# Chunk attention and a wave MLP on one core: per-bank PSUM copies, single matmuls of zeros, more DMA transposes, and a new order of work

## The chip, the cores and the metric

The kernel runs on one core of one Trainium2 chip. The metric is device time in microseconds (us): the time of one launch, median over several runs. A profile of one execution is at hand for the kernel before the change. The engines go by these names: PE (TensorE, matmuls and transposes), PEld (its weight loads), DVE (VectorE), ACT (ScalarE), POOL (GpSimd, which here only issues loads) and SP (SyncE, which issues stores and DMA transposes). PSUM is the memory that PE writes to[...]. SBUF is the working memory.

## What is computed

The inputs q, k and v have the shape (8 batches, 8 heads, 576 tokens, 64). Attention runs within chunks of 64 tokens. Its output x (8, 576, 512) goes through a token-mixing layer and a channel layer:

```
scores = scale * q_c @ k_c.T          # per chunk of 64 tokens, per head
attn   = softmax(scores)
x      = attn @ v_c                   # heads side by side: (8, 576, 512)
theta  = x @ w_theta                  # 512 x 512
zr, zi = x * cos(theta), x * sin(theta)
y      = w_tok_r @ zr + w_tok_i @ zi  # mixing over the 576 tokens of a batch
u      = x + y
out    = u + relu(u @ w_ch)           # 512 x 512
```

## The kernel before

The work goes by pairs of batches, p = 0 to 3. The 2 x 576 tokens of a pair are nine tiles of 128 rows. Tiles 0 to 3 belong to the first batch, tiles 5 to 8 to the second, and tile 4 holds the last 64 tokens of each. Attention and theta go by groups: A is tiles 0 and 1, B is tiles 2 and 3, M is tile 4, C is tiles 5 and 6, D is tiles 7 and 8. The token mixing and everything after it go by single tiles.

The whole program is one hand-written list, ORDER (line 18), which the loop at line 569 walks from left to right. Each entry is step.place.slot, for example `H.1C.2`: theta of pair 1, group C, into PSUM slot 2. An entry such as `W.24.0` is pair 2, tile 4. [...] The steps are these:

- `q`, `k`, `v`: loads of one group, two DMAs each, issued by POOL (lines 174 and 182). They cast from float32 to float16. `lt` and `lc` load w_theta and w_ch, `lw.01` loads w_tok_i, all by POOL. `lw.00` loads w_tok_r by SP, and `cw` casts it on ACT. `init` makes the identity matrix on POOL, `ones` fills constants on DVE.
- `TW` transposes a third of the token weights on PE into two PSUM banks (line 225). `twd` copies part of it out on DVE, `twa` the rest on ACT (line 241).
- `T` transposes q and k of a group on PE into two PSUM banks (line 259). `tq` copies q out on DVE, `tk` copies k out on ACT, or on DVE for group M (lines 277 and 279).
- `S` is the scores on PE (line 290), `e` their exponential on ACT (line 303), `V0` and `V1` are attention times v for four heads each on PE (line 323), `v0` and `v1` the normalisation on DVE into x (lines 335 and 336).
- `X` transposes x on PE (line 354) and `x` copies it out on ACT (line 366). `Xd` (line 375) does both with one DMA transpose, issued by SP.
- `H` is theta on PE (line 388), `g` cosine and sine on ACT (lines 404 and 408), `z` the products on DVE (lines 417 to 426), `zm` two small DMAs on SP that bring the halves of group M to their places.
- `Y` is the token mixing of one tile on PE, nine matmuls of 128 x 512 (line 457). It needs z of the whole batch. `Ya`, `Yb` and `Yc` are parts of it. `y` adds x on DVE (line 465).
- `U` transposes u on PE (line 474), and `u` copies it out on ACT for even tiles and on DVE for odd ones. `Ud` (line 482) does both with one DMA transpose by SP.
- `W` is the channel layer on PE (line 497), `w` its relu and sum on DVE (line 506), `st` two stores by SP (line 521).
- `D` multiplies zeros by zeros on PE into one of two PSUM banks, twice (line 157). Its result is read by nobody.

The pool of x transposes holds three tiles, that of u transposes four, that of loaded q and k seven groups. [...]

Of the kernel before, what the change touches and what calls it, by code (L numbers as in the profile page):

```python
# [10 lines left out]
FP16 = mybir.dt.float16  # L11
# [4 lines left out]


ORDER = """
ones.00 D.00.0 lw.00 cw.00 D.00.1 init.00 D.00.0 D.00.1 q.0M q.0B q.0A D.00.0 k.0M
D.00.1 D.00.0 D.00.1 k.0B TW.00.0 twa.00 k.0A D.00.0 T.0M.1 tk.0M D.00.1 D.00.0 tq.0M  # L20
S.0M.2 e.0M lt.00 T.0B.1 T.0A.2 tk.0A tq.0B D.00.1 tq.0A tk.0B S.0A.2 v.0M V1.0M.1 v.0A
e.0A D.00.0 V0.0M.2 twd.00 S.0B.0 new.00 v1.0M V1.0A.1 v0.0M V0.0A.2 v0.0A v.0B q.1M
v1.0A lw.01 X.0M.2 e.0B V1.0B.0 X.0A.1 v1.0B x.0M H.0M.2 V0.0B.0 x.0A v0.0B q.0C k.1M
v.0C H.0A.1 g.0M X.0B.0 z.0M zm.0M x.0B g.0A TW.02.2 H.0B.0 T.1M.1 twa.02 twd.02 TW.01.2
z.0A Ya.01.1 tk.1M tq.1M g.0B Ya.03.0 twd.01 S.1M.1 k.0C q.0D z.0B q.1B twa.01 Yb.01
T.0C.0 e.1M Yb.03 tq.0C Yc.03 tk.0C S.0C.2 Yc.01 v.1M y.03 k.0D Ya.02.0 e.0C lc.00
V1.0C.1 new.10 V0.0C.0 Yb.02 y.01 v0.0C Yc.02 v.0D v1.0C U.01.1 X.0C.2 u.01 T.0D.0
V0.1M.1 Ya.00.1 Yb.00 x.0C tk.0D y.02 U.02.0 tq.0D v0.1M V1.1M.2 k.1B v1.1M S.0D.1
H.0C.0 u.02 W.02.0 w.02 e.0D V1.0D.2 q.1D V0.0D.1 Yc.00 v1.0D v0.0D g.0C U.03.0 T.1B.2
X.0D.1 X.1M.0 u.03 q.1A y.00 z.0C x.0D W.03.0 w.03 tq.1B x.1M U.00.1 k.1D u.00 H.0D.1  # L30
W.01.1 w.01 tk.1B g.0D z.0D H.1M.0 S.1B.2 k.1A g.1M T.1D.1 tk.1D q.1C v.1B tq.1D e.1B
v.1A W.00.0 k.1C w.00 z.1M Y.05.1 st.01 T.1A.0 tk.1A Y.07.0 v.1D y.05 tq.1A q.2D V0.1B.1
S.1A.2 S.1D.0 e.1D y.07 U.05.1 u.05 Y.06.0 U.07.1 v0.1B e.1A V1.1A.0 y.06 V1.1B.1 T.1C.2
u.07 tk.1C st.02 st.00 v1.1A U.06.0 u.06 tq.1C v1.1B st.03 Y.08.1 X.1B.0 v.1C V0.1A.2
x.1B S.1C.1 W.05.0 V0.1D.0 y.08 v0.1A e.1C v0.1D X.1A.2 x.1A w.05 U.08.1 zm.1M H.1B.1
W.07.0 H.1A.0 g.1B V1.1D.2 w.07 v1.1D Y.04.0 X.1D.1 q.2M z.1B k.2D q.2C g.1A V1.1C.2
T.2D.0 y.04 x.1D z.1A W.06.0 w.06 k.2M tk.2D H.1D.1 v1.1C st.05 u.08 Y.13.0 tq.2D S.2D.2
v.2C g.1D T.2M.0 k.2C y.13 V0.1C.1 Y.10.1 v0.1C X.1C.1 tk.2M tq.2M q.2A e.2D S.2M.0
st.06 T.2C.2 v.2D y.10 st.07 e.2M x.1C new.20 Y.11.0 q.2B v.2M z.1D q.3A W.08.1 tk.2C
k.2B tq.2C k.2A y.11 w.08 S.2C.0 V1.2D.1 U.11.0 e.2C v1.2D H.1C.2 u.11 V0.2D.0 v0.2D  # L40
V0.2M.1 q.3C g.1C U.13.1 v0.2M st.08 Y.12.0 u.13 W.11.1 y.12 X.2D.0 x.2D w.11 V1.2M.1
k.3A V1.2C.2 v1.2M W.13.0 v1.2C U.10.1 V0.2C.1 v0.2C u.10 T.2B.0 st.11 T.2A.2 tk.2A
tk.2B X.2M.1 w.13 tq.2A W.10.1 z.1C U.04.0 u.04 st.13 w.10 H.2D.2 x.2M k.3C tq.2B W.04.0
w.04 H.2M.1 g.2M Y.17.1 v.3C q.3M T.3A.0 X.2C.1 y.17 g.2D v.2B Y.14.0 st.10 z.2M S.2B.2
x.2C tk.3A tq.3A S.2A.1 S.3A.0 y.14 Ud.17 U.12.1 u.12 Y.18.0 y.18 e.2A Y.16.1 k.3M y.16
e.2B W.17.0 v.2A H.2C.1 e.3A w.17 V1.2A.2 v1.2A V0.2A.0 W.12.1 st.04 zm.2M Y.15.0 v0.2A
Ud.14 v.3D w.12 y.15 g.2C V1.2B.2 v1.2B V0.2B.0 v0.2B q.3B X.2A.1 W.14.1 x.2A Ud.18 w.14
st.17 U.16.0 u.16 T.3C.2 X.2B.1 W.16.0 w.16 tk.3C U.15.1 x.2B H.2A.0 u.15 q.3D k.3B
W.15.0 W.18.1 st.12 T.3M.1 k.3D tq.3C z.2C S.3C.2 w.15 w.18 z.2D tq.3M g.2A e.3C st.14
v.3A H.2B.0 Y.27.0 st.16 new.30 v.3M Y.28.1 z.2A tk.3M g.2B y.28 S.3M.2 y.27 z.2B  # L50
V0.3A.1 T.3B.0 Y.26.1 Y.20.0 tq.3B st.18 v0.3A tk.3B Ud.28 V1.3A.0 y.26 e.3M y.20 v1.3A
V1.3M.2 V1.3C.1 v1.3M v1.3C Y.24.1 V0.3C.0 T.3D.2 st.15 Ud.27 S.3B.1 y.24 tq.3D v0.3C
Ud.26 W.26.0 w.26 e.3B W.27.1 v.3B w.27 tk.3D V1.3B.1 V0.3B.0 v0.3B v1.3B S.3D.2 Ud.20
st.27 W.28.0 w.28 Y.21.1 y.21 Xd.3A Ud.21 Y.25.0 V0.3M.0 st.28 v0.3M y.25 e.3D V1.3D.2
V0.3D.1 st.26 Xd.3M Y.22.1 H.3A.0 Ud.24 v0.3D y.22 v1.3D W.21.0 w.21 W.20.1 H.3M.1 g.3A
Y.23.0 Ud.22 w.20 y.23 W.22.1 g.3M Xd.3B st.21 z.3M st.20 H.3B.2 Ud.25 g.3B Xd.3D W.24.0
w.22 w.24 W.25.1 H.3D.0 w.25 Xd.3C z.3B H.3C.1 z.3A g.3C Ud.23 W.23.0 st.22 w.23 z.3C
g.3D zm.3M Y.32.1 y.32 Y.31.0 z.3D Y.30.1 y.31 Y.37.0 st.24 st.25 y.30 st.23 Ud.30 y.37
Y.35.1 W.30.0 y.35 Ud.31 W.31.1 w.30 Ud.32 Ud.35 Ud.37 w.31 st.30 st.31 Y.36.0 W.35.1
y.36 w.35 W.32.0 w.32 st.35 Ud.36 Y.34.1 y.34 Y.33.0 W.37.1 y.33 W.36.0 w.37 Y.38.1  # L60
st.32 Ud.34 w.36 Ud.33 y.38 st.37 W.34.0 w.34 W.33.1 w.33 st.36 st.34 st.33 U.38.0 u.38
W.38.1 w.38 st.38 D.00.0
""".split()


# [1 line left out]
def kernel(  # L67
# [11 lines left out]
    nc = tc.nc  # L79
    B, H, S, D = q.shape  # L80
    DM = H * D
    CH = 64
    P = 128
    NDB = DM // P
    NE = H // 2
# [67 lines left out]

    def idle(p, i, slot):
        ps = psum1("ps_idle", slot)
        for r in range(2):
            nc.tensor.matmul(ps, blank[:, 0:P], blank, start=True, stop=True)

# [42 lines left out]

    def tok_w(k3, slot):
        ps = psum2("ps_wT", slot, FP16)
        for k in range(3):
            kt = 3 * k3 + k
            for tb in range(KT + 1):  # L210
                rows = slice(0, P if tb < KT else CH)
                if tb < KT:
                    at = k * KT * P + (tb // 2) * GT + (tb % 2) * CH
                    to = ps[:, at : at + GT].rearrange("p (c r x) -> p c r x", c=2, r=2)
                    to = to[:, :, 0]
                else:
                    at = 3 * KT * P + k * CH
                    to = ps[:, at : at + CH]
                for h in range(2):
                    if kt < 2 * KT:  # L220
                        ri, jl = kt // KT, kt % KT
                        s0 = (jl // 2) * GT + (jl % 2) * CH + h * P
                    else:
                        ri, s0 = h, KT * P
                    nc.tensor.transpose(
                        to[half[h]],
                        wnat[rows, tb, ri, s0 : s0 + CH],
                        id16[rows, rows],
                    )
        st["wT", k3] = ps  # L230

    def tok_w_copy(k3, r):
        ps = st["wT", k3]
        ks = slice(3 * k3, 3 * k3 + 3)
        most = ps[:, 0 : 3 * KT * P].rearrange("p (k x) -> p k x", k=3)
        if r == 0:
            c = slice(0, GT)
        else:
            c = slice(GT, KT * P)
        eng = nc.scalar.copy if r else nc.vector.tensor_copy  # L240
        eng(out=wT[:, ks, c], in_=most[:, :, c])
        if r == 0:
            eng(
                out=wT[:, ks, KT * P : S],
                in_=ps[:, 3 * KT * P : 3 * S].rearrange("p (k c) -> p k c", k=3),
            )

    def qk_t(p, g, slot):  # L250
        n = 1 if g == "M" else 2
        ps = psum2("ps_qkT", slot, FP16)
        psv = ps.rearrange("p (r w e j c) -> p r w e j c", r=2, w=2, e=NE, j=2)
        t = nats.pop((p, g))
        for w in range(2):
            for e in range(NE):
                for j in range(n):
                    for r in range(2):
                        nc.tensor.transpose(  # L259
                            psv[:, r, w, e, j, :],  # L260
                            t[half[r], w, j, 2 * e : 2 * e + 2, :].rearrange(
                                "s h d -> s (h d)"
                            ),
                            id16[half[r], half[r]],
                        )
        st[p]["ps_qkT", g] = psv

    def qk_copy(p, g, which):
        n = 1 if g == "M" else 2
        ps = st[p]["ps_qkT", g][:, :, which]  # L270
        name = "qk"[which] + "T"
        t = tmp.tile([P, 2, NE, n, CH], FP16, name=name, tag=f"{name}{n}", bufs=n + 1)
        st[p][name, g] = t
        copy = nc.scalar.copy if which and n == 2 else nc.vector.tensor_copy
        if n == 2:
            flat = "p r e j c -> p r (e j c)"
            copy(out=t.rearrange(flat), in_=ps.rearrange(flat))  # L277
        else:
            copy(out=t[:, :, :, 0], in_=ps[:, :, :, 0])

    def scores(p, g, slot):
        n = 1 if g == "M" else 2
        qT, kT = st[p].pop(("qT", g)), st[p].pop(("kT", g))
        ps = psum2("ps_sT", slot)
        psv = ps.rearrange("p (h j e c) -> p h j e c", h=2, j=2, e=NE)
        for j in range(n):
            for e in range(NE):
                for h in range(2):
                    for r in range(2):
                        nc.tensor.matmul(  # L290
                            psv[half[r], h, j, e, :],
                            kT[half[h], r, e, j, :],
                            qT[half[h], r, e, j, :],
                        )
        st[p]["ps_sT", g] = ps

# [306 lines left out]
```

The softmax here doesn't subtract the row's maximum and nothing guards it: scores larger than these inputs give would overflow.

## Time and profile before

| | |
|---|---|
| time, three runs | 213.17, 213.19 and 211.98 us (median 213.17) |
| the profiled execution | 213.03 us, its span 210.7 us |
| granted PE clock, mean over the span | 0.959 |
| busy: PE, DVE, ACT, POOL | 191.4, 123.6, 111.3, 104.4 us |
| loads by POOL (q, k, v) | 120 DMAs, about 0.87 us of POOL each |
| x transposes: by PE and ACT, by DMA | 15, 5 |
| u transposes: by PE and a copy, by DMA | 16, 20 |
| matmuls of zeros | 28 |

The profile is read in this way. Busy times are unions of an engine's instructions, and matmuls are pipelined: a 128 x 512 matmul has a duration of 0.38 us but in a stream one starts every 0.215 us. The span cut into slices shows which engine works when. The chain of waits that ended last is followed back from the last instruction; each of its pieces gives a start, a length and what ran. A table of waits says which instruction stood idle for which other. The table of DMA issues gives the time from issue to landing. Loads run from the start to about 120 us, and in that time the DMA engines are busy nine tenths or more in nearly every slice.

### The profile page before, as it was taken

Reading aid. Unit: us, or ns where it says so; the run is one execution under the profiler, and the core shown is the slowest. Engines: PE = TensorE matmul, PEld = TensorE weight load, DVE = VectorE, ACT = ScalarE, POOL = GpSimd, SP = SyncE. Lnnn points to the kernel's source line nnn. Section 1 sums busy time; section 2 is a strip of 40 time slices with the busy share of each in tenths; the row PEclk is TensorE's granted clock in tenths of the full one; section 3 lists DMA queues with packets and bytes.
Section 4 is the critical chain, followed back from the end, with each engine's and each line's share of the span. In section 5 each row is a group of like instructions: output and inputs, shape, how many; then the busy total and the mean of one; then the engine's idle time right before and its main releaser. Section 6 shows DMA issues by size and latency. Waiting matters only on the chain.

```text
span 210.7 us, 6370 instructions
## 1 busy us (share of the span) xinstructions
PE 191.4 (91%) x2774; PEld 96.7 (46%) x2774; DVE 123.6 (59%) x240; ACT 111.3 (53%) x119; POOL 104.4 (50%) x130
## 2 busy tenths in 40 slices
PE   7678698897989999999999999999899988999981
PEld 2334444353545654555555545545544424444430
DVE  0014644663959675776884447849886365846451
ACT  2525469635886668777567668793260631500010
POOL 8997889988999898987997000000000000000000
PEclk9965579999999999999999999999999999999999
DMA  6999999999999999999999972423428687626875
GB/s 191 189 149 171 186 156 159 162 157 156 150 147 210 218 160 178 153 213 158 169 186 201 190 106 53 104 50 65 91 56 173 125 173 151 151 59 130 174 155 130
DMA packets 136858, 31.36 MB, mean 149 GB/s; under 512 B 129536, under 2 KB 131648, under 8 KB 136832
## 3 DMA queue, kind: packets, MB, share of 16 engines
q0 software_dynamic: 114176, 15.88, 119.6%
q1 hardware_dynamic: 22656, 15.10, 31.5%
q8 instruction: 21, 0.34, 0.7%
q14 instruction: 5, 0.04, 0.1%
HBM read 33.06 MB, written 9.44 MB: 202 GB/s over the span
## 4 chain that ended last, share of the span: by engine, by line
PE 65%; DVE 9%; ACT 9%; DMA 7%; POOL 6%; issue 1%; SPq 0%; POOLq 0%; ACTq 0%
PE ps_y L457 27%; PE ps_theta L388 14%; PE ps_uw L497 13%; POOL qk L174 5%; DMA v<-in_v_dram 4%; PE ps_x L323 3%; DMA xT<-x 3%; ACT kT L277 3%; PE ps_qkT L259 3%; PE ps_sT L290 2%; DVE qT L277 2%; PE ps_xT L354 2%; DVE x L336 2%; ACT xT L366 1%; PE ps_uT L474 1%
## 5 line engine op out<-in xcount | busy, mean ns | idle before, releaser
L457 PEld LDWEIGHTS <-wT 128*128 128x128 f16 (+1 forms) x360 | 30.7, 100 | 34.4 <-issue 0.8
L457 PE MATMUL ps_y<-zr,wT 128*128 128x512 f16 (+1 forms) x180 | 44.4, 381 | 0.0
L457 PE MATMUL ps_y<-zi,wT 128*128 128x512 f16 (+1 forms) x180 | 42.0, 379 | 0.0
L465 DVE TENSOR_TENSOR u<-ps_y,x 128x512 f16<-128x512 f32 x36 | 24.7, 690 | 27.9 <-PE ps_y L457 27.8
L497 PE MATMUL ps_uw<-wch,uT 128*128 128x512 f16 x144 | 36.3, 380 | 1.2 <-ACT uT L491 0.7
L388 PE MATMUL ps_theta<-wtheta,xT 128*128 128x512 f16 x144 | 36.0, 393 | 1.4 <-DMA xT<-x 1.0
L174 POOL DMA_DIRECT2D qk<-in_q_dram x40 | 34.2, 875 | 4.9 <-issue 1.4
L174 POOL DMA_DIRECT2D qk<-in_k_dram x40 | 34.1, 870 | 2.7 <-DMA wnat<-in_moe_w_tok_i_dram 0.8
L182 POOL DMA_DIRECT2D v<-in_v_dram x40 | 34.1, 879 | 2.3 <-DMA qk<-in_k_dram 0.6
L506 DVE SCALAR_TENSOR_TENSOR o<-ps_uw,u 128x512 f32<-128x512 f32 x36 | 24.8, 689 | 15.8 <-PE ps_uw L497 15.5
L404 ACT ACTIVATE cos<-ps_theta,pihalf 128x1024 f16<-128x1024 f32 (+1 forms) x20 | 20.6, 1032 | 21.4 <-PE ps_theta L388 14.9
L303 ACT ACTIVATE eT<-ps_sT 128x1024 f16<-128x1024 f32 (+1 forms) x20 | 18.5, 939 | 16.9 <-PE ps_sT L290 16.8
L336 DVE TENSOR_TENSOR x<-ps_x,recip 128x512 f16<-128x512 f32 (+1 forms) x40 | 25.5, 638 | 1.4
L388 PEld LDWEIGHTS <-xT 128*128 128x128 f16 x144 | 13.7, 100 | 17.9 <-issue 2.1
L497 PEld LDWEIGHTS <-uT 128*128 128x128 f16 x144 | 13.0, 98 | 16.6 <-DMA uT<-u 1.3
L366 ACT COPY xT<-ps_xT 128x1024 f16<-128x1024 f16 (+1 forms) x15 | 13.9, 931 | 12.2 <-PE ps_xT L354 12.1
L277 ACT COPY kT<-ps_qkT 128x1024 f16<-128x1024 f16 x16 | 16.1, 1018 | 7.7 <-DVE qT L277 4.4
L408 ACT ACTIVATE sin<-ps_theta 128x1024 f16<-128x1024 f32 (+1 forms) x20 | 18.7, 937 | 0.0
L491 ACT COPY uT<-ps_uT 128x512 f16<-128x512 f16 x9 | 5.3, 592 | 24.3 <-PE ps_uT L474 24.2
L277 DVE COPY qT<-ps_qkT 128x1024 f16<-128x1024 f16 x16 | 11.0, 688 | 9.3 <-ACT kT L277 6.6
L259 PE MATMUL ps_qkT<-id,qk 64*128 64x64 f16 x576 | 12.8, 196 | 2.1 <-DMA qk<-in_k_dram 1.3
L335 DVE RECIPROCAL recip<-ps_x 128x8 f32<-128x8 f32 (+1 forms) x40 | 7.9, 197 | 10.5 <-PE ps_x L323 10.2
(43 smaller groups left out, 153.5 us busy)
## 6 DMA issues: line engine op xcount, KB each, us to landing
out_dram<-o SPq DMA_DIRECT2D x72, 128.0 KB, 2.4
qk<-in_q_dram POOLq DMA_DIRECT2D x32, 128.0 KB, 6.2
qk<-in_k_dram POOLq DMA_DIRECT2D x32, 128.0 KB, 6.5
v<-in_v_dram POOLq DMA_DIRECT2D x32, 128.0 KB, 6.7
wraw<-in_moe_w_tok_r_dram SPq DMA_DIRECT2D x1, 1152.0 KB, 5.8
wnat<-in_moe_w_tok_i_dram POOLq DMA_DIRECT2D x1, 576.0 KB, 7.7
qk<-in_q_dram POOLq DMA_DIRECT2D x8, 64.0 KB, 6.4
qk<-in_k_dram POOLq DMA_DIRECT2D x8, 64.0 KB, 6.1
```

The source lines that it names most:

```text
L174: nc.gpsimd.dma_start(nats[p, g][rows, which, r], (q, k)[which][b, :, t0 : t0 + n, :].rearrange("h s d -> s h d"),)
L182: nc.gpsimd.dma_start(v16[rows, slot + r, :, 0:D], v[b, :, t0 : t0 + n, :].rearrange("h s d -> s h d"),)
L259: nc.tensor.transpose(psv[:, r, w, e, j, :], t[half[r], w, j, 2 * e : 2 * e + 2, :].rearrange("s h d -> s (h d)"), id16[half[r], half[r]],)
L277: copy(out=t.rearrange(flat), in_=ps.rearrange(flat))
L336: nc.vector.tensor_tensor(out=st[p]["x"][:, j0 : j0 + n, f * NE * D : (f + 1) * NE * D].rearrange("p c (h d) -> p c h d", h=NE), in0=psv[: ...
L388: nc.tensor.matmul(ps[:, j * DM : j * DM + DM], xT[:, j * NDB + db, :], wtheta16[:, db, :], start=(db == 0), stop=(db == NDB - 1),)
L404: nc.scalar.activation(out=cos[:, 0:n].rearrange("p a e -> p (a e)"), in_=pin, func=AF.Sin, bias=pihalf, scale=1.0,)
L408: nc.scalar.activation(out=sin[:, 0:n].rearrange("p a e -> p (a e)"), in_=pin, func=AF.Sin)
L457: nc.tensor.matmul(ps[rows], wT[:, kt, cols], z[:, jz, :], start=(kt == 0), stop=(kt == 2 * KT),)
L465: nc.vector.tensor_tensor(out=u, in0=st[p].pop(("ps_y", j))[:, 0:DM], in1=st[p]["x"][:, j], op=ALU.add)
L497: nc.tensor.matmul(ps, uT[:, db * P : db * P + P], wch16[:, db, :], start=(db == 0), stop=(db == NDB - 1),)
L506: nc.vector.scalar_tensor_tensor(out=o, in0=st[p].pop(("ps_uw", j)), scalar=0.0, in1=u, op0=ALU.max, op1=ALU.add)
```

## The change

Five things change.

First, the copies out of PSUM go by bank. For groups A to D, `tq` now copies the bank of half r = 0 (q and k) on DVE, and `tk` the bank of half r = 1 (q and k) on ACT, into one common tile `qkT`. For group M one DVE copy takes both banks, and its `tk` is gone. The token weights are laid out in PSUM so that `twd` (DVE) reads only the first bank and `twa` (ACT) only the second.

Second, `D` is one matmul of zeros in place of two, and ORDER holds 60 of them in place of 14: 30 before the first `T`, 20 between it and the first `Y` part, one before `W.00`, and nine at the end behind `W.38`.

Third, x of pairs 1 and 2, groups A to D, is transposed by `Xd` in place of `X` and `x` (eight groups). Pair 3 was so before.

Fourth, u of tiles 0, 1, 2, 3, 5 and 6 of pair 1 is transposed by `Ud` in place of `U` and `u`.

Fifth, ORDER is written anew. It starts with groups A and B of pair 0 in place of M; `init` comes after ten loads; `cw` comes after the exponentials of groups A and B, and `TW.00` after the first attention; `lt` comes after 20 loads of q, k and v in place of 12; `lw.01` comes after 24 in place of 20. The other steps are the same in number.

The core of the diff, with ORDER cut to its beginning, a stretch of pair 1 and its end:

```diff
 ORDER = """
-ones.00 D.00.0 lw.00 cw.00 D.00.1 init.00 D.00.0 D.00.1 q.0M q.0B q.0A D.00.0 k.0M
-D.00.1 D.00.0 D.00.1 k.0B TW.00.0 twa.00 k.0A D.00.0 T.0M.1 tk.0M D.00.1 D.00.0 tq.0M
-S.0M.2 e.0M lt.00 T.0B.1 T.0A.2 tk.0A tq.0B D.00.1 tq.0A tk.0B S.0A.2 v.0M V1.0M.1 v.0A
...
+ones.00 q.0A D.00.0 D.00.1 q.0B D.00.0 D.00.1 D.00.0 D.00.1 D.00.0 D.00.1 D.00.0 D.00.1
...
+D.00.1 D.00.0 q.0M D.00.1 D.00.0 D.00.1 k.0A D.00.0 D.00.1 k.0B D.00.0 D.00.1 init.00
+T.0A.0 new.00 T.0B.1 tk.0A tq.0A lw.00 tk.0B k.0M tq.0B S.0A.2 D.00.0 S.0B.0 D.00.1
...
+v.1B V0.1A.1 v0.1A T.1B.0 tq.1B Y.04.1 tk.1B k.1C T.1C.2 tk.1C S.1B.1 e.1B zm.1M y.04
+tq.1C v.1C U.07.0 Xd.1A q.2M u.07 Y.06.1 q.2A U.04.0 V0.1B.0 y.06 V1.1B.2 S.1C.1 W.07.1
+u.04 v1.1B v0.1B Xd.1B U.08.0 u.08 w.07 H.1A.2 q.2C W.08.0 w.08 W.04.1 w.04 e.1C V0.1C.0
+V1.1C.1 Y.05.0 v.1D st.08 st.04 v0.1C k.2A V0.1D.0 g.1A V1.1D.2 v1.1C y.05 U.06.1 Xd.1C
+H.1B.1 U.05.0 u.06 W.06.1 v0.1D T.2A.0 g.1B z.1A k.2C v1.1D tk.2A new.20 w.06 T.2C.2
+H.1C.1 tq.2C st.07 u.05 g.1C Xd.1D z.1B q.2B W.05.1 Y.11.0 k.2M w.05 tq.2A st.06 st.05
+tk.2C v.2A H.1D.1 y.11 Ud.11 v.2M z.1C k.2B Y.10.1 y.10 g.1D S.2C.0 q.2D T.2M.2 W.11.0
...
+W.30.1 Y.38.0 w.30 y.38 Ud.24 W.34.1 W.24.0 w.34 U.38.1 u.38 st.30 W.38.1 w.24 D.00.0
+D.00.0 D.00.0 D.00.0 st.34 st.24 w.38 st.38 D.00.1 D.00.0 D.00.1 D.00.0 D.00.1
 """.split()
...
     def idle(p, i, slot):
         ps = psum1("ps_idle", slot)
-        for r in range(2):
-            nc.tensor.matmul(ps, blank[:, 0:P], blank, start=True, stop=True)
+        nc.tensor.matmul(ps, blank[:, 0:P], blank, start=True, stop=True)
...
     def tok_w(k3, slot):
         ps = psum2("ps_wT", slot, FP16)
...
+        first = ps[:, 0 : 3 * GT].rearrange("p (k x) -> p k x", k=3)
+        middle = ps[:, 3 * GT : 3 * GT + 3 * CH].rearrange("p (k x) -> p k x", k=3)
+        second = ps[:, 1024 : 1024 + 3 * GT].rearrange("p (k x) -> p k x", k=3)
+        for tbs in (range(KT), (KT,)):
...
     def tok_w_copy(k3, r):
-        ps = st["wT", k3]
+        first, middle, second = st["wT", k3]
         ks = slice(3 * k3, 3 * k3 + 3)
...
+            nc.vector.tensor_copy(out=wT[:, ks, 0:GT], in_=first)
+            nc.vector.tensor_copy(out=wT[:, ks, KT * P : S], in_=middle)
         else:
...
+            nc.scalar.copy(out=wT[:, ks, GT : 2 * GT], in_=second)
...
-    def qk_copy(p, g, which):
+    def qk_copy(p, g, r):
         n = 1 if g == "M" else 2
...
+        ps, t = st[p]["ps_qkT", g], st[p]["qkT", g]
+        if n == 1:
+            nc.vector.tensor_copy(
+                out=t[:, :, :, :, 0].rearrange("p r w e c -> p (r w e) c"),
+                in_=ps[:, :, :, :, 0].rearrange("p r w e c -> p (r w e) c"),
+            )
         else:
-            copy(out=t[:, :, :, 0], in_=ps[:, :, :, 0])
+            copy = nc.scalar.copy if r else nc.vector.tensor_copy
+            flat = "p w e j c -> p (w e j c)"
+            copy(out=t[:, r].rearrange(flat), in_=ps[:, r].rearrange(flat))
```

## The prediction

> **What bounds the kernel now.** I read the page's busy shares first, then the chain of waits in order of time, then the table of waits, then the DMA issues by stretch.
>
> ```profile
> PE 191.4 (91%) x2774; PEld 96.7 (46%) x2774; DVE 123.6 (59%) x240; ACT 111.3 (53%) x119; POOL 104.4 (50%) x130
> ...
> PEclk9965579999999999999999999999999999999999
> ```
>
> PE is busy nine tenths of the span; no other engine exceeds six. The second line is the granted clock in 40 slices of 5.3 us: it sags to half in the third to sixth. To see what PE's work is worth at full speed I take the pieces of the chain view in which PE follows PE: `Y` 1.94 us (2.05 for tile 4), `H` 1.73 (0.86 for M), `W` 0.86, `T` 0.57 (0.30), `S` 0.38 (0.20), `V` 0.25 (0.13), `X` 0.34 (0.17), `U` about 0.25, `TW` 1.54 from the timeline. Over ORDER, without zeros, this is 171.7 us. `W.38` ends at 205.9, so PE carries 34.2 us of **overhead** (idle, half clock, zeros). Where it arises: for a step, take its start in the timeline minus the full-speed work that stands before it.
>
> - `H.0M` starts at 25.5 with 5.4 of work before it: 20.1.
> - `S.1M` at 37.7: 23.2. `H.0C` at 50.1: 26.1. `S.1A` at 67.9: 27.3. `Y.17` at 111.9: 29.1. `Y.24` at 148.8: 30.7. `Y.32` at 179.0: 32.9. End: 34.2.
>
> So two thirds lie in the first 50 us, while loads arrive; afterwards PE is the bound and loses 8 us in 155. After `W.38`, 4.8 us remain to the end of the span (relu, store, closing).
>
> Two places show the reader how the losses look:
>
> ```profile
> 14.43 7.94 DMA v<-in_v_dram
> 22.41 0.66 PE ps_x L323 x28
> ...
> 47.35 0.92 ACT kT L277
> 48.29 0.69 DVE qT L277
> ...
> 171.23 3.25 DMA xT<-x
> 174.53 3.63 PE ps_theta L388 x16
> ```
>
> First PE waits for v to land. Then `S.0D` waits for the k copy and, after it, the q copy. Late in the run theta waits for a DMA transpose. The pair of copies is a wait of its own in the table (total us, times, longest):
>
> ```profile
> DVE qT L277 <- ACT kT L277: 6.6, 7, 1.4
> ...
> ACT kT L277 <- DVE qT L277: 4.4, 2, 3.5
> ...
> DVE wT L241 <- ACT wT L241: 3.6, 1, 3.6
> ```
>
> [...] weight loads of the zeros stand 0.43 us apart until 5.44 and 0.21 after; the clock is granted at 0.50 from about 12.7 to 28.7, in a stretch full of gaps. [...] two stores of a tile land in 2.4 us each after the loads, in 5.7 among them.
>
> **The change part by part.**
>
> *PE work removed.* Eight `X` by 0.34 and six `U` by 0.25: 4.2 us, leaving 167.5. PE is the bound from 50 us on, so this counts in full unless the transposes come late. The freed 8 x 1.01 us of ACT copies (line 366), 3 x 0.59 of ACT and 3 x 0.42 of DVE copies (lines 491 and 489) are worth nothing by themselves: ACT is at 53%.
>
> *Copies by bank.* Sizes are unchanged (0.69 on DVE, 1.02 on ACT), but they start together: `T` to `S` is shorter by the 0.69 that stood behind. For M, one copy of some 0.69 replaces two of 0.42. On PE's path I find this pair before `S.0C` and `S.0D` (idle 0.84 and 1.29), and near 107, 117 and 145; I take 1.4 us in 38 to 50, 0.6 in 68 to 112, 0.4 later. In the token weights it frees 1.5 to 3.6 us of waiting on ACT and DVE, partly on the path to the first `Y`.
>
> *The start.* POOL begins loads at 0.75 (before: 1.43, after the identity). Ten loads at 0.86 later `init` costs 0.5. `v.0A` is issued by 11.6, and with 6.7 to land comes near 18.3, not 22.4. But `lt` now stands behind 20 loads: 0.75 + 0.5 + 20 x 0.86 = 18.5, and it took 7.6 from issue to landing (11.45 to 19.05), so `H.0M` cannot start before 26.1: overhead 20.7 there, 0.6 more than before. `lw.01`, four loads later relative to attention, is issued near 23.5 and lands (7.5) near 31; `TW.01` has 10.6 of work ahead, at overhead 21 or more 31.6, so it is just in time. The cast `cw` (2.1 + 0.7 on ACT) was free in the load wait; now `e.0M` stands behind it, ending near 21, and `V1.0M`, `TW.00` and `X.0M` still precede 26.1. So `lt` is what is late next. By `S.1M` I take 23.2 again: the bank copies and a sooner full clock win back the 0.6.
>
> *Zeros.* 30 before the first `T` cost 10 x 0.43 + 20 x 0.215 = 8.6 us and end near 10, before k lands near 12: covered. Twenty among the first steps cost 4.3 us warm, 8.6 cold; between 12 and 26 PE has only 5.4 us of work, so I count nothing; without that cover, up to 8.6. One later: 0.2. Nine behind `W.38`: the first four precede nothing, the next needs the bank that `w` reads until 206.6, then five take 1.1 us, inside the store's 2.4: nothing.
>
> *DMA transposes.* Each `Xd` puts 1.28 us of issue on SP, each `Ud` 1.21: 17.5 us on a queue that spends far more than that waiting between 60 and 120. Behind a waiting `Xd` stand stores, and for them `w`, which has four output tiles; `Ud` too. The stretch is the loaded one:
>
> ```profile
> out_dram<-o SPq DMA_DIRECT2D x16, 128.0 KB, 5.7
> ...
> uT<-u SPq DMA_TRANSPOSE x1, 6.6
> ...
> xT<-x SPq DMA_TRANSPOSE x5, 3.2
> ```
>
> These are stores between 60 and 100, the first `Ud` at 114.6, and all `Xd` of before, which ran after the loads. A loaded `Xd` isn't shown. From below it is 3.2; by ratio of stores 3.2 x 5.7 / 2.4 = 7.6, and I allow 10. I take what load adds to a store, 3.3: 6.5. For `Ud` 5.1 and 6.6 are shown; I take 5.7. Against that stands the PE work between the last `V` and `H`, with 0.9 us per normalisation on the way: 1A 0.9 + 6.5 against 8.25; 1B 1.8 + 6.5 against 8.38; 1C 8.3 against 6.92; 1D 8.3 against 9.01. `Ud.11`: 0.9 + 5.7 against the 4.35 between `Y.11` and `W.11`; `Ud.10` 6.6 against 6.12, covered by 11's stall. Others have 6 us after the loads, or 10. Stalls: 1.4 + 2.25 = 3.6 us. At 3.2 and 5.1, the bound from below: 1.6. At 10 and 6.6, stalls inside another's interval counted once: 10.6.
>
> *Loads.* Their number and 0.87 us each stay; pairs 2 and 3 are issued 5 to 30 us ahead of use, so a few us of DMA time for the transposes cost nothing. If the cover goes, pair 1's loads are nearest (`k.1A` lands near 50 to 53, used at 54).
>
> *Late transposes of pair 3* stay: `Xd.3B` to `Xd.3D` still follow each other on SP; 2.2 us of loss kept.
>
> **Sum.** Overhead 20.7 at `H.0M`; 2.5 to `S.1M`; 1.5 to `H.0C` (2.9 less 1.4); 1.2; then 1.8 - 0.6 + 3.6 = 4.8 for 68 to 112; 1.2 (1.6 less 0.4); 2.2; 1.3: 35.4. With 167.5 and 4.8 the span is 207.7, against 210.7. The profiled execution was 213.03, 2.3 more than its span and 0.1 under the median, so **210.0 us**.
>
> **Rivals.** *Transposes in time and an early full clock.* Stalls 1.6, and the half clock until 28.7 is gone (theta and attention from 25.5 to 30.3 took 2.5 us more than at full speed; I take 1.5): 3.5 less, 206.5. For: sustained zeros at the front. Against: POOL's landings of 6 to 7 us.
>
> *Transposes too late (slower).* At 10 and 6.6 the stalls are 7.0 more: 217. For: the DMA engines show nine tenths until 120, and x's 256 KB are twice u's. It decides from where stalls exceed 6.6, near a loaded `Xd` of 8.2. Its place is `H.1A` to `W.11`, 70 to 100 us.
>
> *A late start.* PE stays at half clock, zeros of 0.43 lie in front of real work, and `lt` lands at 28: 3 to 4 more, 213.5.
>
> *The banks change nothing*, because ACT's 1.02 is what `S` waits for: the 2.4 us counted return, 212.4.
>
> **How the numbers follow.** About 1% is what a measurement can tell from no change. Forecast 0.36 (0.24 of it faster, 0.12 the same); in time and warm 0.24, all faster; late start or no effect of the banks 0.14 (0.02 faster, 0.09 same, 0.03 slower); transposes too late 0.26 (0.03 same, 0.23 slower). Together faster 0.50, same 0.24, slower 0.26. The range 204 to 217 leaves out some 0.08 below and 0.11 above; the forecast's own is 207.5 to 212.5.
>
> **What would show it.** In the changed profile: q and k copies on ACT and DVE that start together; `H.0M` near 26, held by wtheta; the clock at full before 28; `Xd` of pair 1 landing in 6 to 7 us; PE idle before `H.1C` and `W.11`, 1 to 3 us each; overhead near 35. I am wrong if loaded `Xd` take over 8 us, if loads wait for transposes and `T` of pair 1 or 2 waits for k, or if `H.0M` starts after 28.

## The result and the profile after

The changed kernel takes **233.22 us** (median of four runs, 231.06 to 233.91) against 212.6 us before: a ratio of 1.095, 95% interval 1.087 to 1.104. It is slower by a tenth, outside the range of 204 to 217. The profiled execution took 233.91 us, its span is 232.1. Ratios and their intervals, here and below, leave out runs that took over 1.5% longer than the fastest run of the same kernel.

The page of the changed kernel (busy shares, granted clock in 40 slices of 5.8 us, shares of the chain that ended last):

```profile
PE 197.4 (85%) x2654; PEld 95.6 (41%) x2654; DVE 122.0 (53%) x233; ACT 96.5 (42%) x104; POOL 104.2 (45%) x130
...
PEclk9967999999999799599799599999999999999999
...
PE 51%; DMA 25%; ACT 10%; DVE 8%; issue 3%; SPq 2%; POOL 0%; ACTq 0%; DVEq 0%; POOLq 0%
```

PE has fallen from 91% to 85%, and DMA holds a quarter of the chain (7% before). The clock reaches full sooner, and sags again four times between 75 and 133 us. The chain in order of time (start, duration, what) says where:

```profile
69.32 8.85 DMA xT<-x
...
78.21 3.12 PE ps_theta L392 x8
...
86.00 8.13 DMA xT<-x
...
94.17 3.60 PE ps_theta L392 x8
...
102.15 7.08 DMA uT<-u
...
109.28 1.74 PE ps_uw L501 x4
111.02 2.92 PE ps_y L461 x9
...
119.66 10.18 DMA uT<-u
...
129.88 1.89 PE ps_uw L501 x4
131.77 2.79 PE ps_y L461 x9
```

Each line with DMA is a transpose that PE waits out. Over the matmuls behind these four waits the granted clock averages 0.59, 0.50, 0.63 and 0.62, and the first piece behind each takes about twice its time at full speed. At full speed the six PE pieces here take 1.73, 1.73, 0.86, 1.94, 0.86 and 1.94 us: 7.0 us lost at the lower clock. PE's idle time in these four waits and in that of `H.2D` is 2.54, 3.65, 3.54, 5.75 and 2.20: 17.7 us.

The DMA issues between 60 and 100 us (queue, count, KB, median us from issue to landing):

```profile
out_dram<-o SPq DMA_DIRECT2D x11, 128.0 KB, 6.5
qk<-in_q_dram POOLq DMA_DIRECT2D x9, 128.0 KB, 8.5
v<-in_v_dram POOLq DMA_DIRECT2D x8, 128.0 KB, 10.3
qk<-in_k_dram POOLq DMA_DIRECT2D x8, 128.0 KB, 9.5
...
xT<-x SPq DMA_TRANSPOSE x4, 8.9
```

Not only the transposes are late. In the same stretch of the kernel before, stores landed in 5.7 us and the loads in less time too:

```profile
qk<-in_q_dram POOLq DMA_DIRECT2D x11, 128.0 KB, 6.8
v<-in_v_dram POOLq DMA_DIRECT2D x12, 128.0 KB, 6.4
qk<-in_k_dram POOLq DMA_DIRECT2D x12, 128.0 KB, 7.0
```

The last load's issue ends at 135.5 us instead of 114.9 (timeline of the changed kernel, then of the one before):

```profile
133.73 1.76 POOL L183 DMA_DIRECT2D v<-in_v_dram  x2 [0.31 <-DMA qk<-in_q_dram]
```

```profile
114.01 0.88 POOL L182 DMA_DIRECT2D v<-in_v_dram  x1 [0.19 <-issue]
```

POOL's own waits say why; waits of its load instructions for earlier loads of q, k and v sum to 22.6 us, before to 4.0. The largest two (us in total, times, longest):

```profile
POOL qk L175 <- DMA qk<-in_q_dram: 11.2, 7, 3.7
POOL qk L175 <- DMA v<-in_v_dram: 6.8, 5, 2.5
```

**The banks.** In the waits of the changed kernel the two copies of q and k still wait for each other, and its timeline shows them in turn:

```profile
DVE qkT L283 <- ACT qkT L283: 19.5, 7, 13.9
...
ACT qkT L283 <- DVE qkT L283: 8.3, 4, 4.1
```

```profile
69.08 0.68 DVE L283 COPY qkT<-ps_qkT 128x1024 f16<-128x1024 f16 x1
...
69.84 1.93 ACT L283 COPY qkT<-ps_qkT 128x1024 f16<-128x1024 f16 x2 [4.13 <-DVE qkT L283]
...
71.80 0.69 DVE L283 COPY qkT<-ps_qkT 128x1024 f16<-128x1024 f16 x1 [1.30 <-ACT qkT L283]
```

Each starts as the other ends, though they read different banks.

**Overhead** (start of a step minus the full-speed work ahead of it) is 22.8 at `H.0M` (28.2 us), 23.2 at `S.1M`, 24.3 at `H.0C`, 26.9 at `W.07` (74 us), 31.2 at `W.06`, 41.1 at `W.11`, 52.7 at `W.14` (151 us), 58.3 at the end. The loss lies mainly between 74 and 151 us.

### The profile page after: what moved, and what is told of

The parts are those of the page before. It is cut to its first block, busy times and chain, and to the rows that moved or that the text cites. A ratio compares the mean times of both kernels' runs of the same rounds, so it can differ in the third digit from the quotient of the medians.

```text
span 232.1 us, 6142 instructions
## 1 busy us (share of the span) xinstructions
PE 197.4 (85%) x2654; PEld 95.6 (41%) x2654; DVE 122.0 (53%) x233; ACT 96.5 (42%) x104; POOL 104.2 (45%) x130
## 4 chain that ended last, share of the span: by engine, by line
PE 51%; DMA 25%; ACT 10%; DVE 8%; issue 3%; SPq 2%; POOL 0%; ACTq 0%; DVEq 0%; POOLq 0%
PE ps_y L461 23%; DMA uT<-u 11%; PE ps_uw L501 11%; PE ps_theta L392 8%; DMA xT<-x 7%; PE ps_idle L158 3%; DMA qk<-in_q_dram 3%; DMA qk<-in_k_dram 3%; ACT qkT L283 2%; DVE x L340 2%; ACT cos L408 2%; ACT sin L412 2%; PE ps_x L327 2%; DVE qkT L283 2%; PE ps_qkT L259 1%
## 5 line engine op out<-in xcount | busy, mean ns | idle before, releaser
L501 PE MATMUL ps_uw<-wch,uT 128*128 128x512 f16 x144 | 39.4, 404 | 12.0 <-DMA uT<-u 11.1
L461 PEld LDWEIGHTS <-wT 128*128 128x128 f16 (+1 forms) x360 | 31.7, 102 | 37.6 <-issue 4.7
L461 PE MATMUL ps_y<-zr,wT 128*128 128x512 f16 (+1 forms) x180 | 46.0, 392 | 0.0
L392 PE MATMUL ps_theta<-wtheta,xT 128*128 128x512 f16 x144 | 37.2, 404 | 8.4 <-DMA xT<-x 8.4
L408 ACT ACTIVATE cos<-ps_theta,pihalf 128x1024 f16<-128x1024 f32 (+1 forms) x20 | 20.6, 1031 | 30.2 <-PE ps_theta L392 29.3
L283 ACT COPY qkT<-ps_qkT 128x1024 f16<-128x1024 f16 x16 | 16.1, 1015 | 27.9 <-PE ps_qkT L259 19.6
L392 PEld LDWEIGHTS <-xT 128*128 128x128 f16 x144 | 13.7, 102 | 26.7 <-DMA xT<-x 10.2
L283 DVE COPY qkT<-ps_qkT 128x1024 f16<-128x1024 f16 x16 | 10.9, 686 | 19.9 <-ACT qkT L283 19.5
L158 PE MATMUL ps_idle<-blank 128*128 128x512 f16 x60 | 19.4, 460 | 1.4 <-DVE blank L145 1.2
L495 ACT COPY uT<-ps_uT 128x512 f16<-128x512 f16 x6 | 3.5, 587 | 33.1 <-PE ps_uT L478 33.1
L259 PE MATMUL ps_qkT<-id,qk 64*128 64x64 f16 x576 | 12.6, 195 | 4.4 <-DMA qk<-in_k_dram 2.9
L259 PEld LDWEIGHTS <-qk 64*128 64x128 f16 x576 | 10.3, 97 | 9.0 <-issue 4.9
```

Source lines behind the costliest of these rows:

```text
L259: nc.tensor.transpose(psv[:, r, w, e, j, :], t[half[r], w, j, 2 * e : 2 * e + 2, :].rearrange("s h d -> s (h d)"), id16[half[r], half[r]],)
L283: copy(out=t[:, r].rearrange(flat), in_=ps[:, r].rearrange(flat))
L392: nc.tensor.matmul(ps[:, j * DM : j * DM + DM], xT[:, j * NDB + db, :], wtheta16[:, db, :], start=(db == 0), stop=(db == NDB - 1),)
L408: nc.scalar.activation(out=cos[:, 0:n].rearrange("p a e -> p (a e)"), in_=pin, func=AF.Sin, bias=pihalf, scale=1.0,)
L461: nc.tensor.matmul(ps[rows], wT[:, kt, cols], z[:, jz, :], start=(kt == 0), stop=(kt == 2 * KT),)
L501: nc.tensor.matmul(ps, uT[:, db * P : db * P + P], wch16[:, db, :], start=(db == 0), stop=(db == NDB - 1),)
```

## Experiments

Times are medians of all runs; the kernel before was 212 to 213 us beside every one of them.

**1. All fourteen transposes back on TensorE, then one kind alone.** In the new order, each `Xd` or `Ud` gives way to the pair of steps that it replaced, put where a PSUM tile is free:

```
-tq.1C v.1C U.07.0 Xd.1A q.2M
+tq.1C v.1C U.07.0 X.1A.0 x.1A q.2M
...
-H.1D.1 y.11 Ud.11 v.2M z.1C k.2B Y.10.1 y.10
+H.1D.1 y.11 v.2M z.1C k.2B Y.10.1 U.11.0 u.11 y.10
```

> The changed kernel with x of pairs 1 and 2 and u of six tiles of pair 1 transposed on PE again (14 transposes taken from the DMA queue, put back on PE with their copies). Theory LATE (PE waits for transposes that land late among the loads, and its clock drops in the waits): the 23 us of overhead beyond the forecast go, 4.2 us of PE work return: 210 to 215, most likely 211. Rival ORDER (the new order of the rest, the zeros or the copies by bank make it slow): 225 or more.

> Only the eight x transposes go back to PE; the six of u stay on the DMA queue. LATE: the waits before theta (about 8.4 us of PE idle with the clock loss behind them 12) go and those before W stay, though shorter since fewer transposes share the queue: 216 to 223. ORDER: 228 or more.

> Only the six u transposes go back to PE; the eight of x stay. LATE: the two waits before W (9.3 us of PE idle, with the clock loss about 13) go, those before theta stay: 217 to 224. The two halves, e2 and e3, should together give about the whole of e1. ORDER: 228 or more.

Measured: both back 220.62 (ratio 1.039, 1.033 to 1.044); X alone back 224.88, 229.14 and 229.83, too far apart for an interval; U alone back 227.21 (1.067, 1.061 to 1.073). All three missed the ranges. The transposes account for 12.6 of the 20.6 us. By the fastest of its runs X alone gives back 8.3, and U alone gives back 6.0, together a little more than both; whether the two kinds simply add up is not shown. And some 8 us remain with these fourteen back on TensorE.

**2. The same transposes, read by nobody.** As both-back, with the fourteen issued at their places as well, into dead space:

```
+    def x_extra(p, g):
+        t = spare(1024).rearrange("p (a c) -> p a c", c=P)
+        nc.sync.dma_start_transpose(t, st[p]["x"][:, j0 : j0 + 2].rearrange("p a e -> p (a e)"))
```

> X and U are computed on TensorE as in e1_xu_pe (220.6 us), and the same fourteen DMA transposes are issued as well, at the places they have in the changed kernel, into a space that nothing reads. So nothing waits for a transpose, but they still take DMA time from the loads. Theory LATE (the matmuls wait for the transposes' landing; the loads are hardly touched): 219-223, and no idle time of TensorE over 1 us before H.1A, H.1C, W.11, W.13. Theory CROWD (the transposes' descriptors hold up the loads of q, k, v and what follows them): 225 or more, the loads ending near 136 us as in the changed kernel rather than near 115.

Measured: 232.47 (1.097, 1.089 to 1.104), as slow as the changed kernel, with no matmul waiting for any of the fourteen. The last load's issue ends at 135.0. POOL's largest wait for earlier loads of q, k and v without and with them:

```profile
POOL qk L175 <- DMA v<-in_v_dram: 1.9, 2, 1.1
```

```profile
POOL qk L176 <- DMA qk<-in_q_dram: 9.4, 6, 3.8
```

So the presence of the transposes costs, and waiting for their landing is only one form in which it is paid. Where PE paid here, its timeline shows (the idle time ahead of the instruction and what ended it in brackets):

```profile
118.50 0.64 PE L462 MATMUL ps_y<-zr,wT 128*64 128x512 f16 x2 [2.88 <-issue]
```

```profile
152.34 1.89 PE L517 MATMUL ps_uw<-wch,uT 128*128 128x512 f16 x4 [3.43 <-DMA uT<-u]
```

The second is a transpose that both-back has too, now late. The first stands in the middle of a group, waiting for nothing that these views show; it comes back at the same matmuls with 0.9, 1.5 and 2.0 us in the next experiments and not in both-back. The traces also keep each DMA packet, and those of the queue that the page calls `instruction`, some 21 pieces of 16 KB in a run, tell more. One such piece landed at 117.04, 1.46 us before PE went on. The kept traces have 18 pauses of PE over 0.4 us without a releaser, in eleven kernels, and each of them ended 1.36 to 1.74 us after such a piece had landed. In both-back the piece landed at 111.62, and PE passed the same place at 113.3 without a pause. The piece itself took 1.63 us, 1.00 in both-back. That PE had run out of instructions there, because this transfer was late like the others, is an inference from these times and from the queue's name; no run tested it. Behind the pause PE ran slower: the granted clock was 0.50 until 123.8 us and 0.65 until 129.6.

At the end this trace has 12.6 us more overhead than that of both-back. Of these, 2.1 are there at `W.07` (76.8 us), 1.3 of them before the first added transpose. From there to 109 us both grow alike, by 5.0 and 4.9. Then 7.0 come until 130 us, the pause of 2.88 and the lower clock behind it, and 3.6 with the late transpose at 152. The changed kernel lost about as much in other places, so it is partly chance that the two times agree so closely.

**3. Is it the bytes, the small packets, the transposing, or the place?** Three variants of the last: the fourteen moved to later places, meant to be behind the last load (with x of pair 2 as source); plain copies of the same bytes; plain copies in pieces of 256 bytes.

```
-        nc.sync.dma_start_transpose(t, st[p]["u", j])
+        nc.sync.dma_start(t, st[p]["u", j].rearrange("p (b c) -> p b c", c=P))
```

> As e4_xu_pe_added (232.5 us: X and U on TensorE, and fourteen DMA transposes of the same sizes that nothing reads), but the fourteen are issued one by one between about 125 and 160 us, after the loads of q, k and v have ended; their source is x of pair 2. Theory CROWD (they cost because they take DMA time from the loads): 219-224, the last load issued near 119 us as in e1_xu_pe (220.6). Theory QUEUE (they cost because of SyncE's queue and of the stores and transposes behind them, wherever they stand): 229 or more.

> As e4_xu_pe_added, at the same places, but the fourteen are plain copies of the same bytes within SBUF in place of transposes; nothing reads them. Theory BYTES (what costs is the bytes that they move): 229 or more, the last load near 133 us. Theory FORM (the transposing transfers are what costs; the same bytes in long rows are nearly free): 220-224, the last load near 119-122 us.

> As e9_plain_copies (223.9 us), with the same bytes at the same places, but in pieces of 256 bytes, about as long as the packets of the transposes, in place of 2 KB and 1 KB. Theory PACKETS (what takes the DMA time from the loads is the number of small packets): 229 or more, the last load near 130 us or later. Theory TRANSPOSING (the transposing transfer itself is dear): 222-226.

The DMA time in this table is the share of the hardware queue on the page times the span, less the same of both-back (29.9% of 217.5); it is in us of all 16 engines. It adds up the times of single packets. The queue of the loads has 118.3% by the same measure in both-back, so packets overlap, and this is not time in which the engines did nothing else. The page's lines of both-back and of the transposes among the loads:

```profile
q1 hardware_dynamic: 22656, 15.10, 29.9%
```

```profile
q1 hardware_dynamic: 34368, 17.98, 41.2%
```

| added to both-back | us | ratio, interval | DMA time | last load's issue ends |
|---|---|---|---|---|
| nothing | 220.62 | 1.039, 1.033-1.044 | 0 | 118.7 |
| plain copies | 223.86 | 1.057, 1.051-1.063 | 10.7 | 121.1 |
| 256-byte copies | 225.32 | 1.056, 1.052-1.060 | 20.1 | 132.1 |
| transposes from 109 us on | 225.37 | 1.063, 1.056-1.069 | 25.3 | 119.3 |
| transposes among the loads | 232.47 | 1.097, 1.089-1.104 | 30.0 | 135.0 |

Transposing among the loads is what is dear here: the same bytes as plain copies take a third of the DMA time (10.7 us against 30.0) and cost 3 to 4 us instead of 12. Cut to 256 bytes, the size of the transposes' packets (the changed kernel's trace has 11264 more packets of that size than that of the kernel before), they cost 4 to 5, and their ratio does not differ from that of the plain copies. The place matters too: at the later places, 5. In that run the first four were issued from 109.0 to 118.1 us, ahead of the end of the loads' issue, and the loads landed until 133, so the cost of transposes wholly behind the loads is not shown by it. One tempting reading falls with the third row: the span is not simply the end of the loads plus a constant, since there the loads end 13 us late and cost some 5. They are issued far enough ahead for that.

The packets show a difference that the table does not. In the kernel before, a load's packet of at most 256 bytes takes 0.033 us on average (60 to 115 us). At times eight or more packets of at most 256 bytes, those of the loads among them, are under way together for over 0.3 us each. From 20 to 165 us such pauses sum to 9.0 us with the transposes among the loads, in the changed kernel too. With 256-byte copies they sum to 3.8, with plain copies to 1.2, with nothing added to 1.8. Why they arise was not tested. Two more differences are not separated: SP needs 1.2 to 1.5 us to issue one of these transposes and 0.5 to 0.7 for a copy, and the 256-byte copies waited 16.9 us in SP's queue for earlier ones, which wrote to the same dead space.

**4. The transposes in the old order.** The kernel before, its order and copies, with only these eight `Xd` and six `Ud`, each where its operand is ready.

> The kernel before with its own order and its own copies; only the eight X and the six U are moved to DMA transposes, each issued where its operand is ready. Theory TRANSPOSES (they are late and crowd the loads in any order): 222-232, with TensorE idle 2-6 us before theta or the uw products of pair 1. Theory ORDER (the new order is what puts them too close to their readers): 211-217.

Measured: 237.94 (1.118, 1.109 to 1.128), worse than either; TensorE idles 15.9 us before theta for xT alone. The new order is not what makes them late: in the old order the fourteen cost some 25 us, in the new 12.6. Part of the 25 is of another kind: loads of v waited 16.2 us for matmuls of attention, and from 100.3 to 108.9 us hardly a DMA packet was under way.

**5. The banks alone.** The order of the kernel before, with the changed copies.

> The kernel before with its own order, X and U on TensorE; only the copies out of PSUM are by bank, ScalarE and VectorE one bank each. Theory SERIAL (two copies of one PSUM tile still take turns, as the trace of the changed kernel seems to show): 212-214, the second copy of a pair starting after the first has ended. Theory PARALLEL (they run side by side and the gain is hidden in the changed kernel by other losses): 209-211, the two starting within 0.3 us of each other.

Measured: 212.27, ratio 0.999 (0.997 to 1.001). Its row in the waits, and that of the kernel before, agree in every number:

```profile
DVE qkT L281 <- ACT qkT L281: 6.6, 7, 1.4
```

```profile
DVE qT L277 <- ACT kT L277: 6.6, 7, 1.4
```

So the two copies still take turns, though each now reads a bank of its own: VectorE's waits for ScalarE's copy 6.6 us in all, in seven waits, as in the kernel before. In the kernel before, only the PSUM tile was common to both; in the changed one they also write one tile `qkT`. Which of the two would hold them there, and whether two separate PSUM tiles would free them, was not tried.

**6. The zeros.** Those ahead of `T` of pair 1 taken from both-back, and from the kernel before.

> e1_xu_pe (220.6 us) without the 49 products of zeros that stand before T of pair 1. Theory WARM (the zeros bring the full clock some 5-10 us sooner, which is what the start gained): 221.5-225, the clock at half until about 30 us. Theory IDLE (PE waits for the first loads anyway, and the zeros change nothing): 219.5-221.

> The kernel before without the 26 products of zeros ahead of T of pair 1. Theory IDLE (as in e10_no_early_zeros: PE waits for loads at the start, and warmth gained there is lost in the next wait): 211.5-213.5. Theory WARM: 214.5-217, as the first theta and attention of pair 0 then run at half clock.

Measured: 220.01 (1.039, 1.033 to 1.044) against 220.62 with them; and 213.69 (1.003, 1.000 to 1.006) for the kernel before. In both-back the zeros do win something at first: the third full theta starts at 32.21 us, without them at 33.70. At the end nothing of that is left there, and at most 0.6% in the kernel before.

**7. Zeros in the waits.** The changed kernel, with zeros ahead of the five products that wait for a transpose.

> The changed kernel with 76 more products of zeros, 9 to 25 of them ahead of each of the five products that wait for a transpose (H.1A, H.1C, W.11, W.13, H.2D). Theory CLOCK (the waits cost twice: once as idle time and once as half clock in the work after them, some 8 us together): 225-228. Theory LANDING (the loss is the waits alone, and the half clock after them is made good by a later wait): 232-236.

Measured: 235.10 (1.107, 1.100 to 1.114). The granted clock is 1.00 from 24 to 200 us, theta takes 1.89 again, and yet (timeline: start, duration, instruction):

```profile
91.19 6.88 PE L164 MATMUL ps_idle<-blank 128*128 128x512 f16 x16
97.91 1.89 PE L398 MATMUL ps_theta<-wtheta,xT 128*128 128x512 f16 x8
...
110.40 1.02 PE L507 MATMUL ps_uw<-wch,uT 128*128 128x512 f16 x4
...
124.33 5.59 PE L164 MATMUL ps_idle<-blank 128*128 128x512 f16 x25
129.97 1.02 PE L507 MATMUL ps_uw<-wch,uT 128*128 128x512 f16 x4
```

The last two start no earlier than in the changed kernel (109.28 and 129.88). It looks as if time regained in one place were lost in the next wait, but the zeros themselves outlasted the waits. The transposes that the five products wait for had landed at 79.38, 94.65, 110.07, 127.87 and 144.16 us, and the products started at 80.00, 97.91, 110.40, 129.97 and 147.91: 10.1 us late in all. For `W.13` and `H.2D` the landing was 2.0 and 3.4 us earlier than in the changed kernel (129.84 and 147.51); whether the full clock brought that is not shown. So the time speaks neither for nor against a price of the half clock; that would need fewer zeros ahead of `H.1C`, `W.13` and `H.2D`.

**8. Where a transpose is free.** In the kernel before, four steps that come after the last load go to DMA: x of groups A and B of pair 2, and u of tiles 5 and 6 of pair 1 (`Ud.15`, `Ud.16`). First each stands right behind its operand, then the same four stand behind those transposes on SP's queue whose operands are ready sooner. A third version adds `Xd.2C` and `Ud.12`.

```
-zm.2M Y.15.0 v0.2A Xd.2A Ud.14
+zm.2M Y.15.0 v0.2A Ud.14 Ud.18 Ud.16 Xd.2A
```

> The kernel before with X of groups A and B and U of tiles 15 and 16 of pair 2 by DMA transposes, and nothing else changed: these four fall after the last load (115 us). If a transpose costs only where it meets the loads, TensorE loses 1.2 us of work and the time is 211-212 against 212.6 (ratio 0.993-0.998). Rival: their landing is late even there (more than 4 us for X): 213-215.

> As e11_dma_after_loads (218.3 us: before, with X of 2A and 2B and U of 2.15 and 2.16 by DMA transposes), but on SyncE's queue these four stand behind the transposes U of 2.14 and 2.18 and the middle rows of pair 2, whose operands are ready sooner. Theory FIFO (in e11_dma_after_loads what was lost was the wait of those behind a transpose whose operand was not ready): 210.5-212.5, ratio 0.990-1.000. Rival DEAR (each transpose after the loads still costs): 214 or more.

> e13_fifo_mended (212.6 us, ratio 0.998) with two more of pair 2 by DMA: X of 2C, issued near 113 us just ahead of U of 2.17, and U of 2.12, behind it. Theory AFTER (the last loads are in the queues until about 117 us, and from there a transpose costs nothing): TensorE saves 0.6 us more, ratio 0.992-0.997. Theory LOADS (one of them meets the last loads and lands late, and SyncE holds U of 2.17 for it): ratio 1.000-1.010.

Measured: 218.32 (1.024, 1.017 to 1.031), then 212.60 (0.998, 0.996 to 1.000), then 215.30 (1.010, 1.007 to 1.014). SP's timeline in the first and the second of them:

```profile
114.82 9.73 SPq L481 DMA_TRANSPOSE uT<-u  x2
...
125.87 0.59 SPq L430 DMA_DIRECT2D zr<-zmid  x1
...
128.37 1.25 SPq L374 DMA_TRANSPOSE xT<-x  x1
129.73 2.52 SPq L481 DMA_TRANSPOSE uT<-u  x2
```

```profile
116.02 0.58 SPq L430 DMA_DIRECT2D zr<-zmid  x1
...
117.36 5.84 SPq L481 DMA_TRANSPOSE uT<-u  x3
...
125.81 1.23 SPq L374 DMA_TRANSPOSE xT<-x  x1
```

In the first, SP stands at `Ud.16` until its u is there (9.73 us for the pair with it), and the middle rows `zr`, which go out at 116.0 in the second, go out at 125.9; `Ud.14`, behind `Xd.2A`, at 129.7. Mending that queue was worth 5.7 us. The two more of the third, issued from 111.5 us on beside the last loads, cost 2.7 us again. The second is the only version whose whole interval lies below the kernel before, by two parts in a thousand, at the edge of what was measured: of the 1.2 us of TensorE work that it saves less than half arrived (0.2% of 212.9 is 0.5).

**9. The rest of the new order.** Both-back with the xT copies of pair 1 on VectorE.

> e1_xu_pe (220.6 us) with the copies of xT of pair 1 on VectorE in place of ScalarE. Theory SCALAR (what e1_xu_pe still loses against the kernel before lies in 70 to 95 us, where theta waits for ScalarE's copies of xT between its tables, cosines and sines; part of it is owed to putting X back into an order made without it): 215-218.5. Theory ORDER (it is spread over the order and no one engine's copies set it): 219.5-222.

Measured: 222.18 (1.039, 1.033 to 1.045): no better. The 7 to 8 us that both-back loses are spread: its overhead grows by 10.3 us from 52 to 132 us (in the kernel before by 3.3) and by 6.7 to the end (4.8). Part may be owed to putting `X` and `U` back into an order made without them. This stays open.

## Why the prediction was wrong, step by step

- **PE work removed** (4.2 us): right as a count, worth nothing here: with that work on TensorE again, the kernel is 12.6 us faster.
- **The start**: right in sum. Overhead 23.2 at `S.1M`, as forecast, and 24.3 at `H.0C` against 24.7; only `H.0M` came at 28.2 instead of 26.1, and not for `lt`, whose w_theta landed at 26.7. What came last was the copy of its xT on ACT (from 27.5), behind that of the token weights (from 26.8). The zeros were free, as said.
- **Copies by bank**, "they start together": an assumption of the author that no trace had shown, and false, credited with 2.4 us. The rival that the banks change nothing was right, for another reason than the one given. This error was small.
- **DMA transposes, the step that failed.** `Xd` in 6.5 us: measured 8.9 (median of pair 1). `Ud` in 5.7: 7.1 for the first and 10.2 for the one before `W.13`. The bound of 8.2, named as the point from which the slower rival decides, was passed. But that rival's 217 was too low as well. Its stalls were counted step by step against the matmul work that the new order puts between a transpose and its reader, and once each. The trace shows 17.7 us of idle time against 3.6 forecast, and the waits come in series: a late theta holds back the `Y` that stands behind it on PE, and so the next `Ud` (theta at 94.17 us, `Y.11` at 99.41, `Ud.11` from 102.15).
- **"Others have 6 us after the loads, or 10"** failed with it. `W.13` waited 5.75 and `H.2D` 2.20, because loads now were issued until 135.5 and landed until 143; their transposes took 10.18 and 6.23.
- **Loads**, "a few us of DMA time for the transposes cost nothing": the cover of 5 to 30 us ahead of use held for the loads themselves (`T` waited for k 2.9 us in all, before 1.3, and all of it before 16 us, in pair 0), but the size was wrong. It is 30 us of packet time of all 16 engines, on engines that the page had shown at nine tenths, and everything else in the queues pays for it: stores landed in 6.5 us instead of 5.7, loads of v in 10.3 instead of 6.4. That the transposes cost as much when nobody reads them was in no rival.
- **The clock** after a wait was not counted. Seven us lost at a granted clock of 0.50 to 0.63 lie on the chain; what they cost in the end stays open, since the zeros of experiment 7 held PE longer than the waits.
- **The new order** was counted at nothing outside the start, where some 8 us are unexplained.
- The signs named were the right ones in part: a loaded `Xd` took over 8 us, and POOL's loads waited, but no `T` of pair 1 or 2 waited for k. `H.0M` after 28 us came as well, without harm.

## What to carry to other kernels

Before moving work from an engine to DMA, look at what the DMA engines do in that stretch: at nine tenths busy no added transfer was free here, and the transposes cost three to four times what plain copies of their bytes did (12 against 3 to 4 us for fourteen). Price it as DMA time of all queues, not as its landing alone, and follow each late landing through to the next transfer that depends on it. On SP's queue a transfer goes behind those whose operands are ready sooner: here `zr` went out at 125.9 us behind a waiting transpose and at 116.0 ahead of it, and mending that queue was worth 5.7 us.

## What the runs showed of the hardware beyond that

- The granted clock did not always tell PE's speed. In both-back without its early zeros the window from 0 to 30 us shows 1.00, and the four matmuls of the first theta still take 1.89 us (windows view, then timeline):

```profile
0.00:30.00 30.00, 11.67 (x300) 8.36 (x301) 7.29 (x20) 12.37 (x13) 26.23 (x38) 1.00 2.10 166
```

```profile
27.26 1.89 PE L389 MATMUL ps_theta<-wtheta,xT 128*128 128x512 f16 x4
```

  With the zeros the same four take 1.04 us. Read durations beside that line. (The window's columns are length, then busy time and count of PE, weight loads, DVE, ACT and POOL, then clock, DMA share and GB/s.)
- Slow matmuls did not follow the length of a wait alone: in the changed kernel they came after 2.54 us (theta 3.12 us) and not after 2.20 (1.90); with the 256-byte copies not even after 3.75 (`W` 1.04). With the transposes from 109 us on, they came after 0.82 us (theta 3.42 us at 90.88, before the first of them), and in both-back the same wait left theta at 1.89.
